# Token assignment: seven comparisons of the fifteenth column move in front of the counts' copy, nine others behind the last column's turned bids

## The chip, the cores and the metric

The kernel runs on one core of one Trainium2 chip. The metric is the device time of one execution in microseconds, and a version is told by the median over its runs. Beside the runs there is one profiled execution, whose trace the rest of this document reads. Its engines are TensorE (PE; its weight loads have a track of their own, PEld), VectorE (DVE), ScalarE (ACT), GpSimd (POOL) and SyncE (SP, which issues DMAs).

## The reference

Three layers run one after the other: attention, a mixture of experts with a gate for each token, and a second mixture of experts in which each of 8 experts takes exactly 224 of the 1792 tokens. The change touches only how the third layer assigns tokens:

```
logits = x @ w_gate
flat = logits.flatten()
order = np.argsort(-flat)
for idx in order:
    tok, e = (int(idx) // E, int(idx) % E)
    if assigned[tok] >= 0 or counts[e] >= cap:
        continue
    assigned[tok] = e
    counts[e] += 1
for e in range(E):
    mask = assigned == e
    h = np.maximum(x[mask] @ w1[e], 0.0)
    out[mask] = h @ w2[e]
```

With N = 1792 tokens, width 768, 8 experts, inner width 1024 and cap = 224.

## The kernel before, in words

The greedy loop is replaced by phases. In a phase each open token bids its best logit for its best open expert; a token's rank among the bids for the same expert is the number of higher bids (ties broken by position). The tokens lie in columns of 128, one token to a partition. There are 16 columns: 14 (numbers 0 to 13, written NT = 14) hold the tokens in the order of the attention's output, and the fifteenth and sixteenth (numbers 14 = NT and 15 = NTP - 1) hold the two last groups of tokens that the second layer finishes, since their logits come late. `bid` holds one bid for each token and column; `rows` holds each column's bids turned, so that every partition has a column's 128 bids along its free axis. A matrix of comparisons (`g`) says for each token of one column which of the 128 tokens of another column bids less; TensorE multiplies such matrices with the one-hot choice of expert (`ohb`) and so sums the counts.

Three stretches of the first phase follow one another. `count` (line 1792) does columns 0 to 13 against each other, while the last products of the second layer still run; its products go to one PSUM bank `pc` (line 1821), which ScalarE copies to `pcs` (lines 1890, 1891), TensorE turns back (line 1896) and VectorE puts into `w` (line 1900). Then `more` adds the fifteenth column (`one`, line 1704: all tokens against the bids of that column, lines 1701 and 1714 on VectorE, products on line 1720), and issues on ScalarE a part of the other direction. `late` (line 1672) does the sixteenth column: its bids are turned on TensorE and copied by ScalarE to `rows` (lines 1776, 1778), VectorE makes `one` for it, and the other direction for both late columns is divided between the two engines. "The other direction" is: the 128 bids of column 14 (or 15) against each token of columns 0 to 13 (or 0 to 14), one comparison of 128 elements for each of these columns.

`all_scalar` (line 1738) makes such comparisons on ScalarE: one Sign instruction for each column (line 1743), and one more Sign over all of them in place (line 1747), which maps zero and one to one. `all_vector` (line 1723) makes the rest in one VectorE instruction (line 1730). `ON_S = 10, 3` says how many columns ScalarE has: columns 0 to 9 of the fifteenth's 14, and the last 3 of the sixteenth's 15. The fifteenth's matrix is `g14`, the fourth of five buffers; the sixteenth's is the third. When both are complete, TensorE multiplies them (line 1691), first the fifteenth's 14, then the sixteenth's 15, and VectorE adds the sums to `w` (line 1693). `settle` then finds who won, which expert is full and where its tokens lie; GpSimd makes `place` (line 1998), TensorE the table (line 2012), and GpSimd gathers the first expert's tokens by an indirect DMA (`xg`, line 2234), which TensorE turns (line 2245) for the third layer's products (lines 2260 and on).

Each engine runs its own instructions in the order in which the program issues them. That order comes from generators that name an engine, a cost and a ready time before each step, and a planner (`Pace`) that runs them beside the main stream by its own clock. Between them TensorE gets filler products of a constant (`busy_pe`, line 1636) in fixed numbers; their results are used by nothing.

Of the kernel before, what the change touches and what calls it, by code (L numbers as in the profile page):

```python
# [36 lines left out]
def attention(tc, q, k, v, g_q, g_k, w_gate, consts, qkv, hook, emit_pair, emit_batch, extra, nb=NB):  # L37
# [12 lines left out]
    with ExitStack() as ctx:  # L50
# [320 lines left out]
        for step in range(8 * np_ + 16 + LAG1):  # L371
            i, t = divmod(step, 8)
            phase[0] = step
            if i < np_:
                if step == 1:
                    stats(1, 1, (3, 3), act=True)
                if step == 2:
                    while drops:
                        drip()
                    for x in (0, 1):  # L380
                        rows(1, x, nc.vector)
                if step == 16:
                    jobs.append(init)
                if t == 0:
                    start(i)
                    if i + 1 < np_:
                        late = 0 if i else 3
                        chain(cols(i + 1, 0), step + late, ((0, last), (1, first), (1, last)))
                        chain(cols(i + 1, 1), step + max(late + 1, CQ), ((0, last), (1, first), (1, last)))
                    if i % 2 and (i + 3) // 2 < len(groups):  # L390
                        stats((i + 3) // 2, step + 2, ST)
                t0 = 0 if i % 2 else 6
                if t in (t0, t0 + 1) and i + 2 < np_:
                    while t0 and drops:
                        drip()
                    rows(i + 2, t - t0)
                if t == (4 + LAG1) % 8 and i % 2 == (4 + LAG1) // 8 and i // 2 + 2 < len(groups):
                    load(i // 2 + 2)
# [442 lines left out]
def moe1(tc, consts, rt, e0, slot0, xs, wt, qkv, x0, w1, w2, w_gate2, y, assigner):  # L841
# [8 lines left out]
    with ExitStack() as ctx:  # L850
# [347 lines left out]
        def slot(s):  # L1198
# [60 lines left out]
            if more:  # L1259
                turn(s + 1)  # L1260
                split1(s + 1, 1)
                ahead(s)
                if small is not None:
                    early = rg[s + 1]
                    late(s + 1)
                    load1(rg[s + 1])
                    split1(s + 1, 0)
                    split1(s + 1, 1)
                    late2, rg[s + 1] = rg[s + 1], early
                if s + 2 < NSLOT:  # L1270
                    load1(rg[s + 2])
                if nxt is not None:
                    load1(tg[nxt])
# [279 lines left out]
NT = N // 128  # L1553
# [3 lines left out]
class Assigner:  # L1557
# [91 lines left out]
    def early(self, before):  # L1649

        nc = self.tc.nc
        self.cols = NT
        t = yield "v", 0.1, 2.0
        nc.vector.tensor_scalar(self.busy[:, :NT], self.l2[:, :NT, E], -100.0, 100.0, op0=OP.mult, op1=OP.add)
        t, to = yield from self.bids(0, NT, t)
        pl, tb = yield from before()

        def logits():
            yield "v", 0.1, tb
            nc.vector.tensor_copy(out=self.m[:, NT, :], in_=pl)  # L1660
            self.cols = NT + 1
            self.new = yield from self.bids(NT, NT + 1, tb)

        def more():
            self.g14 = self.g[-2]
            yield from self.all_scalar(NT, self.g14, 0, ON_S[0])
            return (yield from self.one(NT, self.g[0], *self.new, False))

        yield from self.count(t, to, logits(), more())
        self.cols = NTP  # L1670

    def late(self):

        nc, L = self.tc.nc, NTP - 1
        one, all_ = self.g[1:3]
        self.cols = NTP

        def earlier():
            yield "v", 1.1, 0.0
            self.below(L, one)  # L1680

        t, to = yield from self.bids(L, L + 1, 0.0, earlier)
        ct, t1 = yield from self.one(L, one, t, to, True)
        yield from self.all_scalar(L, all_, L - ON_S[1], L)
        yield from self.all_vector(NT, self.g14, ON_S[0], NT)
        t = yield from self.all_vector(L, all_, 0, L - ON_S[1])
        for n, g in (NT, self.g14), (L, all_):
            t = yield "p", 0.5, t
            self.busy_pe(1 if n == NT else 4)
            for j in range(n):  # L1690
                nc.tensor.matmul(ct[:, n, :], lhsT=g[:, 128 * j : 128 * j + 128], rhs=self.ohb[:, j, :E], start=False, stop=j == n - 1, skip_group_check=True)
        t = yield "v", 0.2, t
        nc.vector.tensor_tensor(out=self.w, in0=self.w, in1=ct, op=OP.add)
        yield from self.settle(0, 0.0)
# [94 lines left out]
        nc.vector.tensor_tensor(out=oh, in0=eq, in1=over(tm), op=OP.is_equal)  # L1789
        return max(tr.values()), t  # L1790

    def count(self, t, to, logits=None, more=None):

# [18 lines left out]
        def products(i):  # L1814
            j = fin[i]
            t = yield "p", 0.03 + G * 0.055, max(to, tg[j])
            g = self.g[buf[j]]
            free[buf[j]] = t
            for q in range(4):
                x = min(G, C - G * q) * 128  # L1820
                nc.tensor.matmul(  # L1821
                    pc[32 * q : 32 * q + 32, :x],
                    lhsT=self.ohb[:, j, :],
                    rhs=g[:, 128 * G * q : 128 * G * q + x],
                    start=i == 0,
                    stop=i == C - 1,
                    skip_group_check=True,
                )
            return t
# [54 lines left out]
                    yield from logits  # L1884
        for i in range(C - LAG, C):
            t = yield from products(i)
        pcs, x, r = self.pcs, C % G * 128, C // G * 32
        t = yield "s", 0.6, t
        if x:
# [3 lines left out]
        t = yield "p", 0.11 * G, t  # L1893
# [5 lines left out]
        t = yield "v", 0.06 + P * E * 1.05e-3, t  # L1899
# [6 lines left out]
        if more:  # L1906
            w = self.w[:, : self.cols]
            t = yield "v", 0.2, max(t, ta)
# [113 lines left out]
    def before(self, free, t):  # L2022

        nc, c, ts = self.tc.nc, self.c, self.t
        P = self.pad
        f = self.fb[:, :P]
        t = yield "v", 0.1, t
        nc.vector.tensor_scalar(f, self.busy[:, :P], 50.0, None, op0=OP.is_lt)
        t = yield "p", 0.12, t + (0.0 if self.spare else LATER)
        self.busy_pe(8)  # L2030
        pf = self.bank()[:, : 2 * P].rearrange("p (i c) -> p i c", i=2)
        for i, m in enumerate(("ut", "ones")):
            nc.tensor.matmul(pf[:, i, :], lhsT=c[m], rhs=f, start=True, stop=True)

        z = NTP // 2
        t = yield "v", 0.5 + 0.22 * (P - 1).bit_length(), t
        nc.vector.tensor_copy(out=ts[0][:, z : z + P], in_=pf[:, 1, :])
        i = 0
        while 1 << i < P:
            w = 1 << i  # L2040
            nc.vector.tensor_tensor(out=ts[i + 1][:, z : z + P], in0=ts[i][:, z : z + P], in1=ts[i][:, z - w : z + P - w], op=OP.add)
            i += 1
        nc.vector.tensor_tensor(out=free, in0=ts[i][:, z - 1 : z - 1 + P], in1=pf[:, 0, :], op=OP.add)
        return t
# [410 lines left out]
ACT_ONES = 3  # L2455
ACT_COLS = {14: (10, 11, 12, 13), 16: ()}
LOGITS = 2
ON_S = 10, 3
ON_POOL = 4
FEW = 7  # L2460
MANY = {2: 11, 4: 7}
# [59 lines left out]
```

## Time and profile before

| | us |
|---|---|
| median of 3 runs | 1000.49 |
| lowest and highest of them | 999.33, 1007.09 |
| profiled execution, its own time | 997.12 |
| its span in the trace | 995.4 |
| TensorE busy in the span | 964.3 |
| VectorE, ScalarE, GpSimd busy | 674.8, 504.9, 300.8 |

The trace counts time from the start of the span. The stretch of the change lies from about 652 to 681 us: the end of the second layer, the first phase of the assignment, the gather of the first expert's tokens. TensorE's busy time there holds the fillers, so that a busy TensorE is not one that does useful work. A row of the timeline that says "x10" is ten instructions of one form merged, from the first one's start to the last one's end; successive instructions of one engine overlap a little. The bracket at a row's end says how long the engine stood idle before it and whose work ended that.

### The profile page before, as it was taken

The page shows a single profiled execution, that of the slowest core. Times are in us where ns is not written, and L with a number is a line of the kernel's source. Part 1 is how long each engine was busy: PE and PEld are TensorE (multiplying, and loading weights), DVE is VectorE, ACT ScalarE, POOL GpSimd, SP SyncE. Part 2 cuts the span into 40 slices and gives each one's busy share as a digit, 9 for nine tenths or more (in the row PEclk, how much of TensorE's full clock was granted, in tenths as well). Part 3 has the DMA queues.
Part 4 walks back from the last instruction along what each step waited for, and adds up shares of the span by engine and source line. Part 5 has one row for each costly group of instructions (what it writes and reads, how often), then busy time and mean ns, then how long its engine had stood idle before and what let it go on. Part 6 is the DMA issues. An engine that isn't in the chain of part 4 may idle for free. (4 is left out here: it accounts for less than half of the span.)

```text
span 995.4 us, 19414 instructions
## 1 busy us (share of the span) xinstructions
PE 964.3 (97%) x6241; PEld 777.0 (78%) x6241; DVE 674.8 (68%) x1742; ACT 504.9 (51%) x1128; POOL 300.8 (30%) x431
## 2 busy tenths in 40 slices
PE   7999999999999999999999999999999999999996
PEld 6676667677666688888888898756757799999996
DVE  6777878878885664644565644586788887787660
ACT  4787777788785522222352222651224476576651
POOL 4877676666633310001060111100010111210100
PEclk9999999999999999999999999999999999999998
DMA  7677567567466345627631111007751386767631
GB/s 164 147 153 166 142 163 165 139 157 176 100 175 206 107 153 183 216 105 275 212 126 51 34 54 49 17 24 270 281 184 47 115 290 218 261 204 237 218 118 31
DMA packets 81039, 152.58 MB, mean 153 GB/s; under 512 B 14270, under 2 KB 53438, under 8 KB 80768
## 3 DMA queue, kind: packets, MB, share of 16 engines
q1 hardware_dynamic: 75376, 127.63, 43.2%
q0 software_dynamic: 5200, 23.33, 7.2%
q8 instruction: 54, 0.88, 0.4%
q14 instruction: 89, 0.73, 0.3%
q10 hardware_dynamic: 320, 0.00, 0.0%
HBM read 112.27 MB, written 17.44 MB: 130 GB/s over the span
## 5 line engine op out<-in xcount | busy, mean ns | idle before, releaser
L232 DVE TENSOR_REDUCE nm<-sp 112x1 f32<-112x448 f32 x192 | 117.0, 618 | 45.5 <-PE sp L231 45.2
L238 ACT ACTIVATE e<-sp,nm 112x448 f32<-112x448 f32 x192 | 123.1, 641 | 33.8 <-DVE nm L232 29.3
L1053 DVE CUSTOM_DVE_ANT_0 prod<-po,wgb,gt 128x384 bf16<-128x384 f32 x96 | 92.6, 965 | 37.7 <-ACT yr L1277 34.3
L246 PE MATMUL tp<-ident,e 112*112 112x112 f32 x768 | 106.0, 260 | 0.0
L246 PEld LDWEIGHTS tp<-ident,e 112*112 112x112 f32 x768 | 88.1, 133 | 19.4 <-ACT et L252 1.3
L2268 PE MATMUL bank<-xx,w1h 128*128 128x448 f32 x288 | 92.6, 378 | 0.0
L252 ACT ACTIVATE et<-tp 112x448 f32<-112x448 f32 x142 | 77.2, 544 | 30.1 <-PE tp L246 29.9
L230 PE MATMUL sp<-bt,at 128*112 128x448 f32 x188 | 83.3, 443 | 0.0
L259 PE MATMUL op<-et,qkv 112*64 112x448 f32 x384 | 82.8, 552 | 0.0
L966 PE MATMUL pg<-w1h,xh 128*128 128x512 f32 x180 | 75.6, 420 | 4.2 <-ACTq L923 2.2
L989 PE MATMUL po<-w2h,hh 128*128 128x384 f32 x224 | 78.9, 352 | 0.1
L2308 POOL DMA_INDIRECT out_dram<-x,ids x16 | 16.2, 1012 | 200.6 <-ACT x L2307 187.9
L2269 PE MATMUL bank<-xx,w1l 128*128 128x224 f32 x288 | 76.5, 265 | 0.0
L990 PE MATMUL po<-w2l,hh 128*128 128x384 f32 x224 | 75.2, 336 | 0.1
L991 PE MATMUL po<-w2h,hl 128*128 128x384 f32 x224 | 75.2, 336 | 0.0
L967 PE MATMUL pg<-w1l,xh 128*128 128x512 f32 x180 | 72.0, 400 | 0.0
L968 PE MATMUL pg<-w1h,xl 128*128 128x512 f32 x180 | 71.7, 398 | 0.0
L231 PE MATMUL sp<-bt,qz 128*112 128x448 f32 x188 | 69.0, 367 | 0.0
L2300 PE MATMUL bank<-w2h,hh 128*112 128x384 f32 x192 | 66.3, 345 | 0.0
L2302 PE MATMUL bank<-w2h,hl 128*112 128x384 f32 x192 | 64.7, 337 | 0.0
L2301 PE MATMUL bank<-w2l,hh 128*112 128x384 f32 x192 | 64.6, 337 | 0.0
L1089 POOL DMA_INDIRECT y<-yr,ti x11 | 11.4, 1040 | 163.0 <-POOLq L923 119.5
(476 smaller groups left out, 2286.3 us busy)
## 6 DMA issues: line engine op xcount, KB each, us to landing
qkv<-in_moe_w_dram SPq DMA_DIRECT2D x88, 384.0 KB
qkv<-in_moe_w_dram SPq DMA_DIRECT2D x36, 512.0 KB
raw<-in_moe_w_dram SPq DMA_DIRECT2D x24, 512.0 KB
bt<-cut SPq DMA_DIRECT2D x96, 112.0 KB
at<-cut SPq DMA_DIRECT2D x96, 112.0 KB
w1s<-in_moe_w_dram SPq DMA_DIRECT2D x12, 512.0 KB
w2s<-in_moe_w_dram SPq DMA_DIRECT2D x16, 384.0 KB
qkv<-in_v_dram SPq DMA_DIRECT2D x12, 448.0 KB
```

What stands on the lines that cost most here:

```text
L230: nc.tensor.matmul(sp, lhsT=at[:, h, cs], rhs=bt[:, h, :], start=True, stop=False)
L232: nc.vector.tensor_reduce(out=st["nm"][:, n : n + 1], in_=sp, axis=AX.X, op=OP.max, negate=True)
L238: nc.scalar.activation(e, st.pop(("s", n)), AF.Exp, bias=st["nm"][:, n : n + 1], accum_out=st["sm"][:, n : n + 1])
L246: nc.tensor.transpose(tp[:, kc, :], e[:, kc * CP : (kc + 1) * CP], ident[:CP, :CP])
L252: nc.scalar.activation(dst, tp, AF.Copy)
L259: nc.tensor.matmul(st["op"][h * D : (h + 1) * D, :], lhsT=raws[i // 2][:, 2, 2 * (i % 2) + h, kc * D : (kc + 1) * D], rhs=st["et"][:, h, k ...
L966: nc.tensor.matmul(pg, lhsT=xh[:, k, :], rhs=w1h[:, k, fs], start=k == 0, stop=False)
L989: nc.tensor.matmul(po[n], lhsT=hh[:, k, :], rhs=w2h[:, kk, cs], start=kk == 0, stop=False)
L990: nc.tensor.matmul(po[n], lhsT=hh[:, k, :], rhs=w2l[:, kk, cs], start=False, stop=False)
L1053: nc.vector.tensor_tensor_reduce(out=prod, in0=y, in1=wgb[:, cs, e], scale=gt, scalar=init[:, e : e + 1] if init is not None else 0.0, op0 ...
L2268: nc.tensor.matmul(pg, lhsT=h[:, k, fs], rhs=xx[:, k].rearrange("p a c -> p (a c)"), start=k == 0, stop=False)
L2269: nc.tensor.matmul(pg[:, :CAP], lhsT=l[:, k, fs], rhs=xh[:, k, :], start=False, stop=k == KD - 1)
```

## The change

The fifteenth column's ten ScalarE comparisons are split in two: seven (`LEAD = 7`) with a second pass of their own go in front of the copies of the counts to `pcs`, the other three with theirs go to `late`, behind the copy of the last column's turned bids. And ScalarE's share of the sixteenth column's comparisons becomes 6 instead of 3, so that VectorE's becomes 9 instead of 12.

```diff
+        def lead():
+            self.g14 = self.g[-2]
+            yield from self.all_scalar(NT, self.g14, 0, LEAD)
+
         def more():
-            self.g14 = self.g[-2]
-            yield from self.all_scalar(NT, self.g14, 0, ON_S[0])
             return (yield from self.one(NT, self.g[0], *self.new, False))
 
-        yield from self.count(t, to, logits(), more())
+        yield from self.count(t, to, logits(), more(), lead())
         self.cols = NTP
...
         ct, t1 = yield from self.one(L, one, t, to, True)
+        yield from self.all_scalar(NT, self.g14, LEAD, ON_S[0])
         yield from self.all_scalar(L, all_, L - ON_S[1], L)
         yield from self.all_vector(NT, self.g14, ON_S[0], NT)
...
-    def count(self, t, to, logits=None, more=None):
+    def count(self, t, to, logits=None, more=None, lead=None):
...
         for i in range(C - LAG, C):
             t = yield from products(i)
+        if lead:
+            yield from lead
         pcs, x, r = self.pcs, C % G * 128, C // G * 32
...
-ON_S = 10, 3
+ON_S = 10, 6
+LEAD = 7
```

On ScalarE, from the copy of the last logits' tokens (`xtm`) to the sixteenth column's second pass, there stood before (`pcs` is the copy of the counts, `g_11127` the fifteenth column's matrix, `g_11126` the sixteenth's, `x_11102` a constant one):

```order
L1108 ACTIVATE xtm<-px 128x384
L1890 ACTIVATE pcs<-pc 128x256
L1891 ACTIVATE pcs<-pc 96x256
L1743 ACTIVATE g_11127<-rows,bid 128x128 x10
L1747 ACTIVATE g_11127<-g_11127,x_11102 128x1280
L1778 ACTIVATE rows<-bank_11526 128x128
L1743 ACTIVATE g_11126<-rows,bid 128x128 x3
L1747 ACTIVATE g_11126<-g_11126,x_11102 128x384
```

and now stands (line numbers are up by three to five in the changed file):

```order
L1108 ACTIVATE xtm<-px 128x384
L1746 ACTIVATE g_11127<-rows,bid 128x128 x7
L1750 ACTIVATE g_11127<-g_11127,x_11102 128x896
L1895 ACTIVATE pcs<-pc 128x256
L1896 ACTIVATE pcs<-pc 96x256
L1781 ACTIVATE rows<-bank_11523 128x128
L1746 ACTIVATE g_11127<-rows,bid 128x128 x3
L1750 ACTIVATE g_11127<-g_11127,x_11102 128x384
L1746 ACTIVATE g_11126<-rows,bid 128x128 x6
L1750 ACTIVATE g_11126<-g_11126,x_11102 128x768
```

Eight instructions moved ahead of the copies, nothing stands any more between them and the turned bids, and four instructions behind these have become eleven.

On VectorE, from the sixteenth column's one-hot choice to the sum into `w`, the order is the same; before:

```order
L1789 TENSOR_TENSOR ohb_11120<-eq,tm 128x8
L1714 SCALAR_TENSOR_TENSOR g_11125<-rows,bid,tri 128x128
L1730 TENSOR_TENSOR g_11127<-rows,bid 128x512
L1730 TENSOR_TENSOR g_11126<-rows,bid 128x1536
L1693 TENSOR_TENSOR w<-w,bank_11527 128x128
```

and now:

```order
L1792 TENSOR_TENSOR ohb_11120<-eq,tm 128x8
L1717 SCALAR_TENSOR_TENSOR g_11125<-rows,bid,tri 128x128
L1733 TENSOR_TENSOR g_11127<-rows,bid 128x512
L1733 TENSOR_TENSOR g_11126<-rows,bid 128x1152
L1696 TENSOR_TENSOR w<-w,bank_11524 128x128
```

Only the width of the fourth row changed, from 12 columns of 128 to 9. The instructions of TensorE, GpSimd and SyncE and their order are the same as before.

## Rows read from the trace of the kernel before

**Rows 1.** The page's first line.

```profile
span 995.4 us, 19414 instructions
```

**Rows 2.** Chain of waits, 664 to 682 us: start, duration, what.

```profile
668.62 1.18 POOL place L1998
669.84 1.87 PE bank L2012 x16
...
674.68 5.62 DMA xg<-y,ids
...
680.35 0.79 PE bank L2245 x6
```

**Rows 3.** Stretches: length, busy time of PE, PEld, DVE, ACT, POOL, clock, DMA.

```profile
680.00:700.00 20.00, 19.65 (x138) 16.95 (x139) 13.52 (x61) 2.73 (x8) 0.00 (x0) 1.00 0.66 264
```

**Rows 4.** Timeline of ScalarE, 652 to 663 us: start, duration, instruction, idle before.

```profile
652.33 0.48 ACT L1108 ACTIVATE xtm<-px 128x384 f32<-128x384 f32 x1
655.86 0.38 ACT L1890 ACTIVATE pcs<-pc 128x256 f32<-128x256 f32 x1 [3.05 <-PE pc L1821]
656.14 0.37 ACT L1891 ACTIVATE pcs<-pc 96x256 f32<-96x256 f32 x1
656.41 3.02 ACT L1743 ACTIVATE g<-rows,bid 128x128 bf16<-128x128 f32 x10
659.46 1.36 ACT L1747 ACTIVATE g<-g,x 128x1280 bf16<-128x1280 bf16 x1
661.38 0.28 ACT L1778 ACTIVATE rows<-bank 128x128 f32<-128x128 f32 x1 [0.56 <-PE bank L1776]
661.69 0.99 ACT L1743 ACTIVATE g<-rows,bid 128x128 bf16<-128x128 f32 x3
662.71 0.61 ACT L1747 ACTIVATE g<-g,x 128x384 bf16<-128x384 bf16 x1
```

**Rows 5.** Timeline of TensorE, 650 to 670 us.

```profile
651.74 0.61 PE L1821 MATMUL pc<-g,ohb 128*32 128x512 bf16 x8
...
655.69 1.46 PE L1636 MATMUL pg<-ones 128*128 128x512 bf16 x3
656.94 1.06 PE L1896 MATMUL px<-ident,pcs 128*128 128x128 f32 x4
...
659.78 1.46 PE L1636 MATMUL bank<-ones 128*128 128x512 bf16 x6 [0.98 <-DVE w L1909]
661.07 0.27 PE L1776 MATMUL bank<-ident,bid 128*128 128x128 f32 x1
...
664.37 0.53 PE L1691 MATMUL bank<-ohb,g 128*128 128x8 bf16 x15
...
666.37 3.18 PE L1636 MATMUL bank<-ones 128*128 128x512 bf16 x14
```

**Rows 6.** The same view, cut off at 664.6 us.

```profile
664.37 0.38 PE L1691 MATMUL bank<-ohb,g 128*128 128x8 bf16 x9
```

**Rows 7.** Timeline of VectorE, 661 to 665 us.

```profile
661.96 2.35 DVE L1730 TENSOR_TENSOR g<-rows,bid 128x512 bf16<-128x512 f32 x2
664.94 0.29 DVE L1693 TENSOR_TENSOR w<-w,bank 128x128 f32<-128x128 f32 x1 [0.62 <-PE bank L1691]
```

**Rows 8.** VectorE's groups by form, 661 to 665 us: busy us, mean ns | idle.

```profile
L1730 DVE TENSOR_TENSOR g<-rows,bid 128x1536 bf16<-128x1536 f32 x1 | 1.8, 1752 | 0.0
L1730 DVE TENSOR_TENSOR g<-rows,bid 128x512 bf16<-128x512 f32 x1 | 0.7, 684 | 0.0
```

**Rows 9.** Stretches as in Rows 3, for the granted clock.

```profile
620.00:625.00 5.00, 2.77 (x13) 2.22 (x12) 1.62 (x10) 1.05 (x2) 2.00 (x15) 0.93 0.26 16
625.00:630.00 5.00, 5.00 (x22) 3.95 (x22) 2.07 (x10) 0.88 (x2) 1.18 (x6) 0.72 0.22 83
...
660.00:664.00 4.00, 4.00 (x47) 2.24 (x45) 2.64 (x5) 2.70 (x6) 0.00 (x0) 1.00 0.00 0
...
672.00:675.00 3.00, 2.99 (x8) 1.15 (x9) 1.22 (x8) 0.00 (x0) 1.30 (x2) 0.52 0.17 70
```

## The prediction, made before the changed kernel was run

> **What bounds the kernel now.** I read the chain of waits first, then the stretch that the change touches, engine by engine. The chain [rows 2] shows that between 668 and 681 us one thing releases the next: GpSimd's `place`, TensorE's table, the gather of the first expert's tokens (5.62 us from issue to landing), and at 680.35 us the turning of the gathered tokens. From there on TensorE is busy 19.65 of 20 us [rows 3] and goes on like that to the end. So whatever moves the end of the assignment's first phase moves the start of the third layer, and nothing behind it waits that could take the move up.
>
> The phase's end hangs on VectorE's sum into `w` at 664.94 us, which waited 0.62 us for TensorE's products of line 1691 [rows 7]. These began at 664.37 [rows 5], right behind VectorE's comparisons, which ran from 661.96 for 2.35 us, to 664.31 [rows 7]. ScalarE had been done with its comparisons since 662.71 + 0.61 = 663.32 [rows 4]. So VectorE bounds this step, and ScalarE had 0.99 us to spare. Where both begin is set by the turned bids: ScalarE copies them at 661.38, after waiting 0.56 us for TensorE, not for its own ten comparisons, which ended at 659.46 + 1.36 = 660.82 [rows 4]. TensorE turned the bids at 661.07, behind six fillers that had waited for VectorE's `w` of line 1909 [rows 5].
>
> **The change, part by part.** The sum is made against the profiled execution, 997.12 us (its span is 995.4 [rows 1], the rest lies around it); the median of the runs is 1000.49, that is 3.37 above.
>
> *Seven comparisons in front of the copies.* ScalarE was idle there for 3.05 us until the counts' products were complete [rows 4]. Ten comparisons take 3.02 us and three take 0.99, so each further one costs (3.02 - 0.99) / 7 = 0.29, and seven take 0.99 + 4 x 0.29 = 2.15. The second pass takes 1.36 for 1280 elements and 0.61 for 384, which is 0.84 ns an element, so 1.04 for 896. The first can start about 0.10 before its predecessor ends, as the second `pcs` copy did (656.14 against 655.86 + 0.38): at 652.33 + 0.48 - 0.10 = 652.71. They end at 654.86, the pass, which needs them all, 0.03 later and 1.04 long, at 655.93. The copy of the counts, which began at 655.86, begins between 655.83 and 655.93: at most 0.07 late. What hides that is TensorE's three fillers: the turning of the counts starts only behind them, at 656.94, while the copies ended at 656.14 + 0.37 = 656.51 [rows 4, 5]. I count 0; without that cover the 0.07 would go onto the chain in full. The comparisons write a buffer that the count of column 12 reads. That column is the tenth of fourteen in the products' order, four products each, and 36 of them stand before the eight at 651.74 [rows 5], which hold it and are over by 652.35, before 652.71. The lower bound for this part is 0 too: nobody waited for a comparison here.
>
> *Ten comparisons and a pass of 1280 gone from behind the copies.* 4.4 us of ScalarE [rows 4], worth 0: its next instruction waited for TensorE, which in its turn waited for VectorE, and neither moves.
>
> *Behind the turned bids.* All starts at the same 661.69. VectorE does nine columns of the sixteenth's instead of twelve: 1536 elements take 1.752 us and 512 take 0.684 [rows 8], 1.04 ns an element, so 384 fewer save 0.40 and VectorE ends at 663.91. ScalarE does first the fifteenth's last three with their pass, just as long as the three that it did before, to 663.32. Then come six more from 663.22: 0.99 + 3 x 0.29 = 1.86, to 665.08; and a pass of 768, 0.61 + 384 x 0.84 ns = 0.93, from 665.11 to 666.04. Thus ScalarE is now 2.13 us later than VectorE, and 1.73 later than VectorE was before. TensorE's order is the same: fourteen products (the fifteenth's columns 7 to 9 now wait for 663.32; four fillers and 0.5 us of room hide that), then the sixteenth's fifteen, of which nine can go and **six stand and wait for ScalarE**. As before (664.31 to 664.37) TensorE starts 0.06 behind the releaser, at 666.10. Before, the sum into `w` began 0.57 after the first of fifteen products [rows 5, 7]. Fifteen last 0.53 and nine 0.38 [rows 5, 6], 0.025 each, so with nine done ahead the sum begins 0.57 - 9 x 0.025 = 0.35 after 666.10: at 666.45 instead of 664.94. **+1.5 us.** Bounds: 1.3 if the pass can overlap the comparisons by as much as independent instructions do, 1.8 if every instruction pays its full end. The value is nearest to the rows of the same instruction forms, so I keep 1.5.
>
> *What queues behind it.* On TensorE the six and fourteen fillers and the table, on VectorE all of `settle`; GpSimd's `place`, the first expert's number and its weights' loads, and the gather follow from those. ScalarE's own next work waits for `settle`. No DMA is moved. All of the +1.5 therefore reaches 680.35 [rows 2].
>
> A rule weighed here: the rows show no wait for a comparison on ScalarE in this stretch, so cutting its block of comparisons into earlier and later pieces has nothing to release. [...]
>
> **Sum:** 997.12 + 1.5 = 998.6 for an execution like the profiled one, and 1000.49 + 1.5 = **1002.0 us** for the median. Chance of this case: 55%.
>
> **Rivals.**
>
> 1. *The new wait costs TensorE its clock (22%).* TensorE's fillers and the nine products end near 664.75, and it then stands idle for some 1.35 us until 666.10. In the records an idle 0.98 us [rows 5] was followed by full clock (660 to 664, 1.00), but 2.23 idle us (620 to 625) by 3.5 us at the lower of the two levels (0.93 and 0.72 as means over 5 us each), and another such stretch stands at 672 [rows 9]. The new wait lies between, nearer to the harmless one. If the clock falls, it falls on the fillers behind the wait. [...]
>
> 2. *Not slower: the gather takes the delay up (12%).* If what ends the gather is the load on the DMA engines and not its own issue, 680.35 stays though the issue comes 1.5 later. For it: 5.62 us is long for one gather [rows 2]. Against it: the weights' loads that share the engines are asked for by the number of the expert and behind the gather on GpSimd, so they move along. It decides if the gather's span shrinks to 4.1 us or less. Time: 1000.5.
>
> 3. *Not slower: the split works as meant (5%).* [...] Time: 1000.49 - 0.4 = 1000.1.
>
> 4. *The front seven start late (6%).* If the buffer is released only with the last of the counts' products, shortly before the fillers at 655.69 [rows 5], they end 0.03 + 2.15 + 1.04 = 3.2 later, at 658.9, and the copies start 3.0 late with the whole chain behind them: 1000.49 + 3.0 + 1.5 = 1005.0.
>
> **The numbers.** The predicted time is the likeliest case, 1002.0. The range reaches down to rival 3's 1000.1 less the 1.2 by which the lowest run lies under the median, 998.9, and up to rival 4's 1005.0, which takes in rival 1's upper bound. One per cent, about what a measurement of this kernel can tell from no change, is 10 us; every case here is within it. 2% for faster and 3% for slower are left for what no case holds, so 95% for the same.
>
> **What would show it.** In the changed profile: the front seven at 652.7 to 654.9 and the counts' copy at 655.9, no later; VectorE's second comparison about 1.35 us long; ScalarE's last pass ending near 666.0; TensorE's products of the sixteenth column broken after nine, and the rest waiting for ScalarE; the sum into `w` 1.5 us later against the turned bids' copy (3.56 us before). A sum into `w` at the old distance would refute the forecast; a lower clock right behind the wait would speak for rival 1, a gather of 4.1 us for rival 2.

## The result and the profile after

The changed kernel took **1006.91 us** in the median (1002.85 to 1015.31) against 999.69 us of the kernel before beside it (997.11 to 1007.09): a ratio of 1.0069 (1.0045 to 1.0094). The direction was forecast, and a time within 1% of no change too; the size was not. 1.5 us were forecast, the medians differ by 7.2, and 1006.91 lies 1.9 us above the range. Two later comparisons of the same kernel gave 1.0032 (1.0011 to 1.0053) and 1.0064 (1.0038 to 1.0090); the first of these alone would leave room for 1.5.

The profiled execution took 1002.85 us (before 997.12); it is the fastest of the nine. Its span:

```profile
span 1001.1 us, 19417 instructions
```

That is 5.7 us above [rows 1]. Where they are is read by following the chain from one landmark to the next, in distances, since everything ahead of the change already stands 0.51 later in this execution. ScalarE first, to be held against [rows 4] (start, duration, instruction, idle before):

```profile
652.84 0.48 ACT L1108 ACTIVATE xtm<-px 128x384 f32<-128x384 f32 x1
653.21 2.14 ACT L1746 ACTIVATE g<-rows,bid 128x128 bf16<-128x128 f32 x7
655.39 1.04 ACT L1750 ACTIVATE g<-g,x 128x896 bf16<-128x896 bf16 x1
656.34 0.36 ACT L1895 ACTIVATE pcs<-pc 128x256 f32<-128x256 f32 x1
...
660.88 0.28 ACT L1781 ACTIVATE rows<-bank 128x128 f32<-128x128 f32 x1 [3.92 <-PE bank L1779]
661.06 0.97 ACT L1746 ACTIVATE g<-rows,bid 128x128 bf16<-128x128 f32 x3
662.06 0.62 ACT L1750 ACTIVATE g<-g,x 128x384 bf16<-128x384 bf16 x1
662.59 1.85 ACT L1746 ACTIVATE g<-rows,bid 128x128 bf16<-128x128 f32 x6
664.46 0.93 ACT L1750 ACTIVATE g<-g,x 128x768 bf16<-128x768 bf16 x1
```

The seven and their pass lie ahead of the counts' copy, which stands 3.50 behind the copy `xtm`, hardly other than before (3.53). Behind the turned bids the last pass ends at 664.46 + 0.93 = 665.39, and VectorE has long been done (its timeline):

```profile
661.46 1.95 DVE L1733 TENSOR_TENSOR g<-rows,bid 128x512 bf16<-128x512 f32 x2
665.79 0.29 DVE L1696 TENSOR_TENSOR w<-w,bank 128x128 f32<-128x128 f32 x1 [2.38 <-PE bank L1694]
```

From the copy of the turned bids to the sum into `w` ("copy to `w`" from here on) it is now 665.79 - 660.88 = 4.91, before 664.94 - 661.38 = 3.56 [rows 4, 7]. TensorE, to be held against [rows 5]:

```profile
663.78 0.37 PE L1694 MATMUL bank<-ohb,g 128*128 128x8 bf16 x9
665.45 0.30 PE L1694 MATMUL bank<-ohb,g 128*128 128x8 bf16 x6 [1.30 <-ACT g L1750]
665.62 2.72 PE L1636 MATMUL bank<-ones 128*128 128x512 bf16 x6
668.20 3.58 PE L1636 MATMUL bank<-ones 128*128 128x512 bf16 x14
...
673.20 1.89 PE L1636 MATMUL bank<-ones 128*128 128x512 bf16 x8 [0.31 <-issue]
...
678.54 0.80 PE L2250 MATMUL bank<-ident,xg 112*128 112x112 f32 x6
681.81 0.79 PE L2250 MATMUL bank<-ident,xg 112*128 112x112 f32 x6 [2.47 <-DMA xg<-y,ids]
682.44 2.48 PE L2109 MATMUL bank<-rows,g 128*128 128x77 f32 x12
...
691.97 0.27 PE L1779 MATMUL bank<-ident,bid 128*128 128x128 f32 x1
```

and the same view of the kernel before, beyond [rows 5]:

```profile
672.01 3.49 PE L1636 MATMUL bank<-ones 128*128 128x512 bf16 x8 [0.32 <-issue]
...
678.90 0.74 PE L2245 MATMUL bank<-ident,xg 112*128 112x112 f32 x6
680.35 0.79 PE L2245 MATMUL bank<-ident,xg 112*128 112x112 f32 x6 [0.71 <-DMA xg<-y,ids]
680.98 1.47 PE L2104 MATMUL bank<-rows,g 128*128 128x77 f32 x12
...
687.21 0.60 PE L1776 MATMUL bank<-ident,bid 128*128 128x128 f32 x4
```

Three things differ. The six products wait 1.30 us for ScalarE, as forecast. Behind them the fillers run slow (the first six take 2.72 us, before 1.46). And at the second turning (that of the second half of the gathered tokens) TensorE, which before came late (eight fillers took 3.49) and waited 0.71 us, now comes early (they take 1.89). The gather is issued 1.2 later, but so do the eight fillers begin 1.2 later (673.20 against 672.01); what they no longer take opens the wait. TensorE stands idle for 2.47 us, and the twelve products behind take 2.48 instead of 1.47. The chain of waits of after, to be held against [rows 2], has the slow fillers directly ahead of the table, and the gather:

```profile
668.34 3.44 PE bank L1636 x14
671.78 1.10 PE bank L2017 x16
...
675.88 5.89 DMA xg<-y,ids
```

The granted clock by stretches of after (length, busy time of PE, PEld, DVE, ACT, POOL, clock, DMA; compare [rows 9]) shows both slow stretches:

```profile
665.00:670.00 5.00, 4.55 (x20) 1.87 (x21) 3.58 (x20) 2.12 (x6) 0.19 (x1) 0.66 0.01 3
670.00:682.00 12.00, 9.21 (x59) 4.88 (x57) 10.22 (x48) 1.18 (x3) 2.98 (x4) 1.00 0.58 162
682.00:690.00 8.00, 8.00 (x41) 7.81 (x40) 0.67 (x6) 0.79 (x2) 0.00 (x0) 0.57 1.03 417
```

Of the 1000 slices of 1 us in this profile 973 read 1.00, 18 read 0.50 and 9 lie between, so the lower level is 0.50. A mean of 0.57 over 8 us is then 6.9 us at the lower level (2 x 0.43 x 8; 6.84 by the slices), with TensorE busy throughout, on the first expert's products that the chain hangs on. From the second turning to the next phase's first turned bids it is 691.97 - 681.81 = 10.16, before 687.21 - 680.35 = 6.86: **3.30 us, more than half of the loss, 16 us behind the change.**

The account of the profiled pair: +0.51 ahead of the change; -1.01 from `xtm` to the turned bids (8.04 instead of 9.05, because before the fillers there ran at the lower clock, 0.50 over 656 to 658, and in after at 1.00; in a later execution of the changed kernel in which they ran at 0.50 too, it was 9.08, so this gain is luck); +1.35 from there to `w`; +0.61 from `w` to the second turning (16.02 instead of 15.41: the gather is issued 0.34 later behind `w`, and takes 5.89 instead of 5.62); +3.30 behind it; +0.94 in all the rest, most of it a single wait of 0.82 of TensorE for VectorE in a later phase, at 834.68. Together 5.70.

### The profile page after: what moved, and what is told of

Its sections match the earlier page's. It is cut to its first block, busy times and chain, and to the rows that moved or that the text cites. A ratio compares the mean times of both kernels' runs of the same rounds, so it can differ in the third digit from the quotient of the medians.

```text
span 1001.1 us, 19417 instructions
## 1 busy us (share of the span) xinstructions
PE 966.0 (96%) x6241; PEld 779.2 (78%) x6241; DVE 677.2 (68%) x1742; ACT 505.6 (51%) x1132; POOL 302.0 (30%) x431
```

## The experiments

The theory after the result: the delay of 1.35 us matters little by itself; with it the gather's wait is open, and it is the lower clock behind *that* which costs. Rivals: the new 1.30 wait starts the loss; the front seven do it; the larger share does it. Each ratio is to the kernel before, run beside it on the same chip (medians 998.35 to 1000.09), with its 95% interval.

**The gather's wait filled.** The change and eleven fillers for TensorE between the two turnings:

```
             if n == g == 0:
                 asn.busy_pe(16)
                 asn.spare = None
+            if n == 0 and g == 2:
+                asn.spare = px0
+                asn.busy_pe(11)
+                asn.spare = None
```

> The changed kernel with 11 more filler products on TensorE between the turning of the first expert's first and second half of gathered tokens, where its trace shows an idle 2.47 us and then 7 us at the lower clock. Theory A (the change's own 1.3 us, and TensorE's clock, which falls after that idle and slows the first expert's products by 3 to 4 us): the idle shrinks under 0.5 us, the clock stays full from 682 to 690 us, and the time falls by about 3.5 us against the changed kernel, to a ratio near 1.003 against before. Theory B (the fall of the clock is a companion of this one trace and the rest of the loss sits in late comparisons or elsewhere): ratio stays near 1.007.

999.92 us, ratio 1.0010 (0.9989 to 1.0032). TensorE and the clock:

```profile
666.68 0.30 PE L1694 MATMUL bank<-ohb,g 128*128 128x8 bf16 x6 [1.30 <-ACT g L1750]
...
680.00 2.54 PE L1636 MATMUL bank<-ones 128*128 128x512 bf16 x11
682.89 0.79 PE L2254 MATMUL bank<-ident,xg 112*128 112x112 f32 x6 [0.34 <-DMA xg<-y,ids]
683.52 1.47 PE L2109 MATMUL bank<-rows,g 128*128 128x77 f32 x12
```

```profile
682.00:690.00 8.00, 7.66 (x58) 7.11 (x57) 2.70 (x17) 0.79 (x2) 0.00 (x0) 1.00 1.02 409
```

The new wait is still there, and the delay with it; with the gather's wait covered the clock stays full behind it (1.00) and the loss is gone.

**The gather's wait opened in the kernel before.** Its sixteen fillers ahead of the turnings halved:

```
-                asn.busy_pe(16)
+                asn.busy_pe(8)
```

> The kernel before, with 8 instead of 16 filler products ahead of the first turning, so that TensorE runs out of work some 1.8 us earlier while the gather is under way; nothing of the change is in it. Theory A: idle of about 2.5 us before the second half's turning, then several us at the lower clock on the first expert's products, and 3 to 4 us more than before (ratio 1.003 to 1.004), though the gather itself lands as early as before. Theory B: the fillers only fill, ratio 1.000.

1000.80 us, 1.0032 (1.0010 to 1.0054): slower by 2.4 us, the size that the theory gives. But the profiled execution does not show its cause:

```profile
676.73 0.79 PE L2245 MATMUL bank<-ident,xg 112*128 112x112 f32 x6
679.91 0.79 PE L2245 MATMUL bank<-ident,xg 112*128 112x112 f32 x6 [2.38 <-DMA xg<-y,ids]
680.54 1.47 PE L2104 MATMUL bank<-rows,g 128*128 128x77 f32 x12
```

Idle 2.38 us, and the products behind it take no longer than at the clock of 1.00 (1.47 for twelve, as in the kernel before). (This execution had slow fillers just ahead, near 672, as the kernel before has: seven from 671.65 on take 2.73 us, 0.39 each, where the eight of after take 1.89, 0.24 each.) An open wait there is thus not enough in every execution, and what made these runs slower is not shown.

**The front seven with the old share**, and **ten in front with it**:

```
-ON_S = 10, 6        -ON_S = 10, 6
+ON_S = 10, 3        +ON_S = 10, 3
                     -LEAD = 7
                     +LEAD = 10
```

> The change with ScalarE's share of the sixteenth column left at 3 instead of 6; seven of the fifteenth's still go in front. Theory A: ScalarE ends its comparisons about 0.5 us behind VectorE's instead of 2.1, the sum into w comes about 3.8 us after the turned bids' copy (3.56 before, 4.91 with the change), so about 0.25 us is lost there; whole time within 2 us of before unless TensorE's clock falls all the same. Rival (the comparisons in front cost the time): still 5 to 7 us slower than before.

998.24 us, 0.9997 (0.9976 to 1.0018). The seven in front neither cost nor bring anything that can be measured. The copy of the turned bids stood at 661.88, the sum into `w` at 665.52: 3.64.

> All ten comparisons of the fifteenth column in front of the counts' copies, ScalarE's share of the sixteenth left at 3; nothing but these three behind the turned bids. Theory A: behind the turned bids the distance to the sum is 3.56 us as before, but the copies of the counts start about 1.2 us late (3.02 + 1.36 us from 652.7), of which TensorE's fillers hide 0.2 to 0.4, so 0.8 to 1.0 us are lost in front. Rival (the front costs nothing): no loss at all, ratio 1.000.

999.36 us, 1.0011 (0.9982 to 1.0039). Ten reach past the fillers' cover. TensorE, at the turning of the counts:

```profile
656.02 0.70 PE L1901 MATMUL px<-ident,pcs 128*128 128x128 f32 x4 [1.14 <-ACT pcs L1895]
```

It waited for ScalarE, and from `xtm` to the turned bids it took 8.41 instead of 8.04: 0.4 lost, where 0.8 to 1.0 were expected.

**The larger share alone**, in the kernel before:

```
-ON_S = 10, 3
+ON_S = 10, 6
```

> The kernel before with one edit of the change alone: ScalarE's share of the sixteenth column is 6 instead of 3; all ten of the fifteenth's stay where they were, behind the counts' copies. Theory A (the loss needs the fifteenth's last three behind the turned bids as well): ScalarE ends its six and their pass about 2.85 us after the copy of the turned bids, VectorE its nine after 2.25, the sum into w comes 3.5 to 3.7 us after that copy (3.56 before, 4.91 with the change), TensorE waits under 0.6 us there, and the time is that of before (ratio 0.999 to 1.001). Rival (the larger share costs by itself): ratio 1.003 or more.

999.35 us, 1.0009 (0.9985 to 1.0032). TensorE:

```profile
662.34 0.30 PE L1691 MATMUL bank<-ohb,g 128*128 128x8 bf16 x6 [0.22 <-ACT g L1747]
```

Six of the sixteenth's on ScalarE are harmless (copy to `w` 3.52) as long as three of the fifteenth's do not stand ahead of them.

**The change without its front part**: the seven stand behind the counts' copies, where the ten stood, and three and six follow the turned bids.

```
         def more():
+            self.g14 = self.g[-2]
+            yield from self.all_scalar(NT, self.g14, 0, LEAD)
...
-        yield from self.count(t, to, logits(), more(), lead())
+        yield from self.count(t, to, logits(), more())
```

> The change without its front part: the seven comparisons stand behind the counts' copies, where the ten stood before; behind the turned bids all is as in the change (three of the fifteenth's, then six of the sixteenth's on ScalarE). Theory A (the work behind the turned bids costs all of it, the front nothing): sum into w about 4.9 us after the turned bids' copy, ratio 1.005 to 1.008 like the change. Rival (the front part has a share, by moving TensorE's products and with them the clock): ratio 1.001 to 1.003.

1003.62 us, 1.0044 (1.0020 to 1.0067): as slow as the change, with the front part gone. Copy to `w` is 4.91, and TensorE:

```profile
681.06 1.02 PE L2248 MATMUL bank<-ident,xg 112*128 112x112 f32 x6 [2.52 <-DMA xg<-y,ids]
681.88 2.71 PE L2107 MATMUL bank<-rows,g 128*128 128x77 f32 x12
...
716.92 0.51 PE L2248 MATMUL bank<-ident,xg 112*128 112x112 f32 x3 [2.73 <-DMA xg<-y,ids]
```

The second expert's gather now came late as well. The same comparison timed the change again, and with the first wait alone filled:

> The changed kernel itself once more, on the same chip as the two others and with another profile. Theory A: ratio 1.005 to 1.009, mean granted clock of the timed runs near 0.985 against 0.991 to 0.992 for before; in the profile an idle time of about 2.4 us ahead of the second turning wherever the fillers before it ran at full clock. If the first timing had a share of chance in it: 1.002 to 1.004.

1002.86 us, 1.0032 (1.0011 to 1.0053); TensorE idled 3.04 us ahead of the second turning. The edit for the first wait:

```
-                self.busy_pe(1 if n == NT else 4)
+                self.busy_pe(1 if n == NT else 10)
```

> The changed kernel with fillers in the first of its two idle times only: 10 instead of 4 ahead of the sixteenth column's products; the second, at the gather, stays open. If the first idle time is the root (it pulls the clock's fall forward to 665 us, the fillers behind it then run at full clock and end early, and the gather is uncovered), the time falls most of the way, to a ratio of 1.002 to 1.003. If the open gather does it whatever comes before, the ratio stays at 1.005 to 1.007 and TensorE idles about 2.5 us ahead of the second turning.

1003.14 us, 1.0034 (1.0013 to 1.0056), beside 1.0032 unfilled: no gain. TensorE:

```profile
683.30 0.79 PE L2250 MATMUL bank<-ident,xg 112*128 112x112 f32 x6 [2.70 <-DMA xg<-y,ids]
683.93 2.25 PE L2109 MATMUL bank<-rows,g 128*128 128x77 f32 x12
```

The first wait is not the cause. With both filled (those ten and the eleven):

> The changed kernel with fillers in both of TensorE's new idle times: 6 more ahead of the sixteenth column's products (10 instead of 4) and 11 between the two turnings of the first expert's tokens. If the clock's fall came from these idle times, the rest is the chain's own 1.3 us: ratio 1.001 to 1.002, mean granted clock of the timed runs at or above before's, as in the run with the gather's fillers alone (1.001). If the first idle time (1.30 us) matters by itself, this run is 1 us or more faster than that one; if not, the two agree.

1000.53 us, 1.0020 (0.9999 to 1.0041): no better than the gather's fill alone. And six fillers there in the kernel before:

> The kernel before with 6 fillers between the two turnings and nothing of the change. In its trace TensorE idles 0.71 us there, in others of its executions perhaps more. If a fall of the clock behind the gather is what lifts some runs of before from 996 to 1003 us, the median falls by 1 to 2 us (ratio 0.998 to 0.999) and the slowest runs by more; if it has no part in before's spread, the six cost 0.6 us where they outlast the gather (ratio 1.0005).

1000.13 us, 1.0019 (0.9998 to 1.0039): the gain that I expected is not there. Where the wait is short already (0.71), there is nothing to cover.

**A delay that has nothing to do with the change.** The kernel before, with nine of VectorE's comparisons done twice:

```
         t = yield from self.all_vector(L, all_, 0, L - ON_S[1])
+        t = yield from self.all_vector(L, all_, 0, 9)
```

> The kernel before with none of the change, but with the same delay made on VectorE: nine of the sixteenth column's comparisons are computed a second time, 1.35 us, so that the sum into w comes 4.9 us after the turned bids' copy as with the change. Theory A (any 1.3 us in this chain does it): the fillers between 672 and 676 us run at full clock, TensorE idles 2.4 us or more ahead of the second turning, several us at the lower clock follow on the first expert's products, and the ratio equals the change's in this batch (1.003 to 1.007). Rival (ScalarE's work itself, or TensorE's interrupted products): no fall behind the gather, ratio 1.001 to 1.002.

1004.02 us, 1.0044 (1.0021 to 1.0066). Copy to `w` is 4.96. TensorE, and the clock:

```profile
666.02 0.56 PE L1692 MATMUL bank<-ohb,g 128*128 128x8 bf16 x15 [1.66 <-DVE g L1731]
...
674.02 1.89 PE L1636 MATMUL bank<-ones 128*128 128x512 bf16 x8 [0.31 <-issue]
...
682.95 1.38 PE L2246 MATMUL bank<-ident,xg 112*128 112x112 f32 x6 [2.82 <-DMA xg<-y,ids]
684.12 2.71 PE L2105 MATMUL bank<-rows,g 128*128 128x77 f32 x12
```

```profile
683.00:690.00 7.00, 7.00 (x32) 6.85 (x33) 0.48 (x5) 0.90 (x2) 0.00 (x0) 0.51 1.03 417
```

The same picture with ScalarE as in the kernel before: eight fillers at 1.89, the gather's wait open, the lower clock (0.51) on the products. The delay does it, whichever engine makes it. Beside it, on one chip, the change and the change with the eleven fillers once more:

> The changed kernel once more, beside the two others of this batch on one chip. The first timing gave 1.0069, the second 1.0032; if chips differ in it, this is one more sample, expected between 1.003 and 1.007.

> The changed kernel with 11 fillers between the two turnings, as before (1.001 then), now on the same chip as the unaltered change. Theory A: 2 to 5 us faster than that, ratio 1.000 to 1.002. Rival: within 1 us of it.

1006.12 us, 1.0064 (1.0038 to 1.0090), without the fillers; 999.90 us, 1.0012 (0.9988 to 1.0036), with them: 6.2 us by eleven matmuls whose products nobody reads. The clock of the first and of the second:

```profile
683.00:690.00 7.00, 7.00 (x31) 6.78 (x31) 0.00 (x0) 0.42 (x2) 0.00 (x0) 0.51 1.03 417
```

```profile
683.00:690.00 7.00, 6.95 (x53) 6.91 (x54) 1.58 (x13) 0.79 (x2) 0.00 (x0) 1.00 1.03 365
```

**A version meant to be faster**: seven in front, the fifteenth's other seven behind the counts' copies, four of the sixteenth's behind the turned bids (`ON_S = 14, 4`), six fillers at the gather:

```
         def more():
+            yield from self.all_scalar(NT, self.g14, LEAD, NT)
...
-        yield from self.all_scalar(NT, self.g14, LEAD, ON_S[0])
```

> A version built on the findings: seven of the fifteenth's comparisons in front of the counts' copies, all its other seven right behind these copies, where ScalarE idles 3.9 us in the changed kernel; behind the turned bids only 4 of the sixteenth's on ScalarE and 11 on VectorE, and nothing of the fifteenth's; 6 fillers between the two turnings. From the rows: ScalarE needs 1.28 + 0.03 + 0.72 us behind the turned bids' copy, VectorE 0.3 + 0.1 + 1.62, so the sum into w comes about 2.7 us after that copy (3.56 before, 4.91 with the change): 0.85 us gained in the chain. With the clock kept as in before the time falls by 1 to 2 us, ratio 0.998 to 0.999; if the shorter chain only lets TensorE wait longer for the gather, 1.000.

998.26 us, 1.0000 (0.9978 to 1.0022). Copy to `w` fell to 3.26, by 0.3 instead of 0.9, because TensorE is next. VectorE:

```profile
661.05 1.62 DVE L1733 TENSOR_TENSOR g<-rows,bid 128x1408 bf16<-128x1408 f32 x1
663.74 0.29 DVE L1696 TENSOR_TENSOR w<-w,bank 128x128 f32<-128x128 f32 x1 [1.07 <-PE bank L1694]
```

VectorE is done at 662.67 and waits for TensorE, whose products could start only at 663.18, behind its own four fillers. No version beats the kernel before measurably.

## Why the prediction was wrong

*What bounds the step; the front seven; the split behind the turned bids: right.* The first comparison began 0.37 behind the copy `xtm` (0.38 forecast), the pass took 1.04 (1.04), the counts' copies stood 0.03 earlier behind `xtm`, the six products began 0.06 behind ScalarE's last pass (0.06) and the sum 0.34 behind them (0.35). The distance from the turned bids grew by 1.35 (1.5); the 0.15 is that ScalarE's first comparison began 0.18 behind the copy instead of 0.31. With the gather covered, the medians differ from before by 1.55, 1.55 and, with both waits filled, 2.15 us (ratios 1.0010, 1.0012 and 1.0020, none apart from 1): near the 1.5 that the chain alone was forecast to cost.

*Ten comparisons gone from behind the copies, worth 0: slightly off.* In [rows 5] the fillers at 655.69 ran at the lower clock (0.50 over 656 to 658), and the turned bids came after ScalarE was done. In two experiments of the old order with the clock at 1.00 in every slice from 650 to 660 (the larger share alone, the delay on VectorE) the copy of the turned bids stood right behind the ten's pass, 8.18 and 8.21 behind `xtm` against 8.04 in after, and 8.18 also with the halved fillers: the ten cost 0.14 there. At full clock the front seven are not quite free either: the counts' copy stands 3.33 behind `xtm` in the run without them and 3.50 with them, and the copy of the turned bids 7.93 and 8.04.

*What queues behind it: the step that failed.* "All of the +1.5 therefore reaches 680.35" holds as far as it goes: 1.35, and 0.61 more, reached the second turning. But the step puts everything behind that point at nothing, as if TensorE went on there at the clock of 1.00 of [rows 3]. It did not: +3.30 lie there. The wait just ahead, 0.71 before, has no place in the prediction's sum; it became 2.47. [rows 2] and [rows 5] come from an execution in which the stretch at the lower clock near 672 [rows 9] made eight fillers 1.6 us longer, and that filled most of the gather's wait. All nine profiles with the delay (after and eight experiments) lack that stretch (clock 1.00 over 670 to 681); all seven without it (before and six) have one that begins at 670 to 673 (down to 0.50 in six of them, fillers at 0.39 each in that of the halved fillers). The delay moved these fillers and the gather alike; the wait opened because the fillers ran at full clock.

*Rival 1 had the cause and the wrong place.* It asked whether the new 1.35 us of idle time would cost the clock, on fillers. The author's estimates of the price were 1.3, and 2.4 if all fourteen ran slow (1004.4, rival 1's upper bound): one filler took 3.18 / 14 = 0.23 at the clock of 1.00 and (656.94 - 655.69) / 3 = 0.42 in the slow stretch [rows 5], and 0.29 of room stood ahead of the table. No run shows either sum. In after, and in two of the five others that have this wait of 1.30, the clock did fall behind it (0.66 over 665 to 670), and it cost little, as the work there is filler: the table began 5.65 to 5.84 behind `w` instead of 4.89, and the gather was issued 10.00 to 10.08 behind it instead of 9.74, so 0.3 us went on. The same wait of 1.30 was followed by a fall in three profiles and by none in three (1.00 over 665 to 670). The wait to price was the next one on TensorE, at the gather. There, with the delay and no cover, the idle time was 2.47 to 3.04 us and the first expert's products behind it ran at the lower clock (0.50) in six profiles of six; with cover (idle at most 0.58) in none of three (1.00). The price is 3.30 in the profiled pair; from the second turning to the next phase's first turned bids it took 10.1 to 10.2 us in those six, and 6.8 to 6.9 in the other ten. From the second turning to the end of the span it was 319.3 to 322.4 us in those six, and 314.9 to 316.4 in nine of the other ten.

*What stays open.* Why a delay of 1.35 us removes the fall near 672, and why the halved fillers' 2.38 us of idle time, behind such a fall, was followed by none. And the rest of the 6.2 us that the eleven fillers gave back. The second expert's gather was late in four of the six (TensorE idle for 1.38 to 2.73 us), and from the next phase's first turned bids to the end these four took 309.6 to 312.2 us, the two others 309.1 and 309.3, nine of the ten without the loss 308.1 to 309.5. But in the tenth, ten in front with the old share, that gather was late too (1.99, and 311.8 to the end) without the delay, so its part in the loss is not shown. The mean granted clock over an execution was 0.986 without and 0.9915 with the fillers (medians), which is 11 us more at the lower level of 0.50 (0.0055 x 2 x 1000) and up to 5.5 us of time; where these all lie was not followed.

The other rivals fell: the gather did not take the delay up (5.89 against 5.62), the split did not gain (1.35 us lost, where rival 3's 1000.1 counts 0.4 gained), and the front seven were not late. The split had nothing to release: the front seven alone gave 0.9997.

## What to carry to other kernels

A delay on the chain is priced by following it to the next places where TensorE waits, and there by the work that stands *behind* the wait: a clock fall on fillers cost 0.3 us here, one on products 3.3, about half of its stretch of 6.8. Fillers counted by hand cover only as long as they run: a cover that comes from a stretch at the lower clock, visible as one filler group with almost twice its usual time per instruction (here 3.49 / 8 = 0.44 us against 1.89 / 8 = 0.24), is no cover to build on. Whoever changes something in front of them counts them anew, at full clock, at the wait that has real products behind it.

## What was not expected of the hardware

An idle 2.5 to 3.0 us of TensorE ahead of dense work was followed, in all six profiles with the delay and no cover, by 6.8 us at the lower clock level of 0.50 (6.82 to 6.84 by slices of 1 us) although TensorE was busy all through them (in the last two such profiles 0.51 over 683 to 690, 7.00 us busy of 7.00). The stretches near 655 and 672 in the kernel before were half as long, 3.4 us each (2 x 0.21 x 8, from the stretches of the kernel before, as in [rows 3]):

```profile
653.00:661.00 8.00, 6.57 (x49) 3.68 (x49) 6.02 (x18) 4.93 (x13) 0.00 (x0) 0.79 0.09 34
670.00:678.00 8.00, 7.68 (x38) 3.79 (x37) 4.68 (x28) 0.00 (x0) 2.01 (x3) 0.79 0.51 132
```

A stretch at the lower clock can be worth something: the one near 672 fell on eight fillers and kept the wait behind them at 0.71 us, which was followed by full clock (1.00 over 680 to 700 [rows 3]).
